# A GLU and linear-attention kernel on one core: the opening in a written order, with products of four blocks first

## The chip, the cores and the metric

One core of a Trainium2 chip runs the whole program. The metric is the device time of one execution in microseconds; lower is better. The core has five instruction streams: TensorE (PE, with its weight loads as PEld), VectorE (DVE), ScalarE (ACT), GpSimd (POOL) and SyncE (SP), which here only issues DMAs. Each stream runs its instructions strictly in order and waits on semaphores of the others.

## The reference, cut to what matters

```python
S, D, H, F = 2048, 1024, 32, 3584                  # float32 throughout
xn = layernorm(x)                                  # mean and variance over D, no weights
# branch A: linear attention with a learned feature map (per head, 32 wide)
q, k, v = split(xn @ wqkv)
phi_q = concat(softmax(q @ w_phi), softmax(-(q @ w_phi)));  phi_k = the same of k
o = (phi_q @ (phi_k.T @ v)) / (phi_q @ sum(phi_k) + 1e-6)
s = o @ wo
# branch B: gated linear unit
h = silu(xn @ w1) * (xn @ w3)
g = silu(h @ w2)
out = x + s * g
```

## The kernel before

The program begins with branch B's first product, xn against w1 and w3. It has two token halves of 1024 tokens; w1 and w3 are cut into 28 blocks of 128 columns (`NF`). One token half against one column block is a **block** k (0 to 55; 0 to 27 are the first half). Each block is a 2 by 2 matrix product (two groups of 512 tokens by two halves of the 1024 features, against w1 and w3), done in Winograd's form with seven products instead of eight. The A operands are A11, A12 (the features of the first 512 tokens), A22, and the sums S1 to S4 of the four quarters; the B operands are B11, B21, B22 and the sums T1 to T4 (`ORDER`).

Every operand is held as two fp32r parts, the rounded value (high, a cast on ACT) and the rest (low, a subtraction on DVE): `split`, L93 and L94 in the trace. A product is 12 matmuls of 128x512 (`PASSES`: high by high, high by low, low by high, for four slices of the features). So nothing can be multiplied before ACT has made its high parts and DVE its low parts.

PSUM has three kinds of banks for the products: b (A11, S2, S3, A22 of a block), a (A11's partner A12) and c (S1, S4); `evict` takes them out on ACT and DVE. A fourth kind, tag `tr`, serves the turns and folds.

**The opening** must make all seven A operands of the first half out of eight x tiles: load (`load_x`, L189), statistics (`stats`, L195 and L196, then `rstd`: a square root on ACT and five small DVE steps), normalization in place (`norm`, L214), **turns** (`turn`: four transposes on PE into PSUM, L219, copied out by ACT, L224), sums (`a_sums`, L231 to L237 on DVE), splits. Tiles 0 to 3 give A11 and A12, tiles 4 to 7 the other quarters.

**Folds** (`fold`, L248) multiply the transposed wk and wq with the block-diagonal w_phi (`bd`), so that later the features come out of one product. There are 32; each is a load (`load_w`, L241), four narrow matmuls on PE, an ACT copy and a store to DRAM (L312, L313). They need neither x nor DVE. 22 of them stand in the opening (`first_folds`), ten are side work.

A scheduler orders the opening; from step 4 of the product list `seq` the program's own order holds (`in_order`). Steps are products. `stage` sets at which step a block's B quarters are loaded and summed on POOL (`b_sums`, L129 and L130, then two more subtractions), `LEAD` splits an operand four steps ahead of its product, and `at`, `side_x`, `side_fold`, `side_kv` and `side_store` hang side work on steps: the second half's x, the remaining folds, the weights of branch A. The pool `q` of 11 rooms of 512 KB passes from x tiles to B operands.

The first products before are

```python
seq[:10] = [(0, "A11"), (0, "A12"), (1, "A11"), (1, "A12"), (0, "S2"), (0, "S1"), (0, "S3"), (0, "S4"), (1, "S2"), (0, "A22")]
```

Of the kernel before, what the change touches and what calls it, by code (L numbers as in the profile page):

```python
# [8 lines left out]
F = mybir.dt.float32  # L9
# [19 lines left out]
def tile_kernel(ctx: ExitStack, tc: tile.TileContext, x, wkT, wqT, wv, wphi, wo, w1, w3, w2, out):  # L29
# [116 lines left out]
    BANKS = {"a": 1, "b": 3, "c": 1}  # L146
# [51 lines left out]
    def rstd(mv):  # L198

        sd = small.tile([P, 4, 2], F, name="sd")  # L200
        var = mv[:, :, 1]
        nc.scalar.activation(sd[:, 0], var, AF.Sqrt, bias=eps_t)
        nc.vector.reciprocal(sd[:, 1], sd[:, 0])
# [12 lines left out]
    def turn(half):  # L216
        pt = ps.tile([P, 4, P], F, name="pt", tag="tr", bufs=3)
        for k in range(4):
            nc.tensor.transpose(pt[:, k, :], half[:, k * P:(k + 1) * P], ident)  # L219
        return pt  # L220
# [23 lines left out]
    def fold(wr, c):  # L244

        pw = ps.tile([P, 4, P], F, name="pw", tag="tr", bufs=3)
        for g in range(4):
            nc.tensor.matmul(pw[:, g, :], wr[:, g], bd[:, 4 * c + g, :], start=True, stop=True)  # L248
        return pw
# [9 lines left out]
    def b_operands(rw, bo):  # L259
        b11, b21, b12, b22 = (rw[:, a, h] for a in range(2) for h in range(2))  # L260
        t2 = work.tile([P, 512], F, name="t2", tag="w")
        b_sums(b11, b12, b22, t2)
        yield
        for _, _, n in ORDER:
            src = {"B11": b11, "B21": b21, "T2": t2, "T1": b11, "T3": b12, "B22": b22, "T4": b21}[n]
            bo[n] = quad("bo")
            split(bo[n][:, 0], bo[n][:, 1], src.rearrange("p (k n) -> p k n", n=P))
            if n == "B11":
                nc.gpsimd.tensor_sub(b11, b22, t2)
            elif n == "B21":  # L270
                nc.gpsimd.tensor_sub(b21, b21, t2)
            yield


    phi_raw = flat(blk("phi")[:, :2]).rearrange("p (g f) -> p g f", f=DH)
    nc.sync.dma_start(phi_raw, wphi.rearrange("(g p) f -> p g f", p=P))
# [12 lines left out]
    for n in ("B11", "B21", "B22", "B12"):
        b_load(1, rws[1], n)  # L290
# [3 lines left out]
    for j in range(4):  # L294
        sl = slice(32 * j, 32 * j + 32)
        nc.gpsimd.tensor_copy(bd[sl, :, sl], phi_raw[sl, :, :])
    b_gen = b_operands(rws[0], bo)
    next(b_gen)

    def first_split(n, q, src):  # L300
        sl = slice(q * P, (q + 1) * P)
        split(ao[n][:, 0, :, sl], ao[n][:, 1, :, sl], src)

    at_fold = 0

    def first_folds(n):
        nonlocal at_fold
        for _ in range(n):
            wT, k, c, d = folds[at_fold]
            wr = early_w.pop(0) if early_w else load_w(wT, k, c, work.tile([P, 4, P], F, name="wr", tag="w"))  # L310
            pw = fold(wr, c)
            nc.scalar.copy(wr, pw)  # L312
            nc.sync.dma_start(d, flat(wr))  # L313
            at_fold += 1
# [3 lines left out]
    for t in range(4):  # L318
        stats(mvs[t // 2], t % 2, xs[t])
    for p in range(2):  # L320
        sd = rstd(mvs[p])
        for j in range(2):
            norm(mvs[p], sd, j, xs[2 * p + j])
    for q in range(4):
        raw[q]["A11"] = raw_x(turn(xs[q][0]))
        first_split("A11", q, raw[q]["A11"])
        if q == 1:
            next(b_gen)
# [12 lines left out]
    next(b_gen)
    for q in range(4):
        if q % 2 == 0:
            sd = rstd(mvs[2 + q // 2])
            for j in range(2):
                norm(mvs[2 + q // 2], sd, j, xs[4 + q + j])
        raw[q]["A21"] = raw_x(turn(xs[4 + q][0]))
        raw[q]["A22"] = raw_x(turn(xs[4 + q][1]))
        a_sums(raw[q], nc.vector)
        first_split("S2", q, raw[q]["S2"])  # L350
        first_split("S1", q, raw[q]["S1"])
        if q == 2:
# [149 lines left out]
    FIRST_STEP, HALF = 7, 7 * NF  # L502
    for i in range(4, 8):
        side_x(i, FIRST_STEP + 16 * (i - 4))
    for m in range(at_fold, len(folds)):
        side_fold(m, FIRST_STEP + 6 * (m - at_fold))
    for m in range(9):
        side_kv(m // 4, m % 4, FIRST_STEP + 62 + 11 * m)
# [37 lines left out]
    def stage(k):

        c, r = 7 * k - 4, raw_of(k)
        if k > 1:
            for n, ahead in (("B11", 10), ("B12", 8), ("B22", 6), ("B21", 4)):  # L550
                at(c - ahead, lambda n=n: b_load(k % NF, rws[k % 2], n), sums)
        at(c - 3, lambda: b_sums(r["B11"], r["B12"], r["B22"], wk[4]), sums)
        at(c - 2, lambda: nc.gpsimd.tensor_sub(r["B11"], r["B22"], wk[4]), sums)
        at(c, lambda: nc.gpsimd.tensor_sub(r["B21"], r["B21"], wk[4]), sums)

    def operand(k, n):

        r = raw_of(k)
        src = {"B11": r["B11"], "B21": r["B21"], "T2": wk[4], "T1": r["B11"], "T3": r["B12"], "B22": r["B22"], "T4": r["B21"]}[n]
        bos[k, n] = quad("bo")  # L560
        split(bos[k, n][:, 0], bos[k, n][:, 1], src.rearrange("p (k n) -> p k n", n=P))

    def evict(step, k, an, pb):
# [3 lines left out]
        h0, u0, u1, h1, even = h0s[k % 2], wk[2], wk[3], wk[f % 2], wk[0]  # L567
        if an == "A11":
            nc.scalar.copy(h0, pb)  # L569
# [24 lines left out]
    for k in range(1, 2 * NF):  # L594
        stage(k)

# [17 lines left out]
    for step, (k, an) in enumerate(seq):  # L614
        if step == 4:
            in_order(ENG.PE, ENG.Activation, ENG.DVE, ENG.Pool, ENG.SP)
        tb, f = divmod(k, NF)
        for do in before.pop(step, ()):
            do()
# [5 lines left out]
        for kk in range(4):  # L625
            for u, w in PASSES:
                nc.tensor.matmul(bank, bt[:, w, kk], aos[tb][an][:, u, kk], start=an in ("A11", "A12", "S1") and n == 0,  # L627
                                 stop=LAST[b] == an and n == 11, skip_group_check=True)
                n += 1
        for do in sums.pop(step, ()):  # L630
            do()
        if step + LEAD < len(seq):
            k2, an2 = seq[step + LEAD]
            if k2 and (k2, OPERAND[an2]) not in bos:
                operand(k2, OPERAND[an2])
        for do in after.pop(step, ()):
            do()
        with tc.high_priority() if step < 4 else nullcontext():
            evict(step, k, an, bank)
# [709 lines left out]
```

## Time and profile before

| | us |
|---|---|
| median of 3 runs (lowest, highest) | 2362.84 (2361.11, 2365.02) |
| profiled execution, its time | 2365.4 |
| profiled execution, its span from first to last instruction | 2363.2 |
| PE busy / DVE / ACT / POOL in the span | 2331.2 / 1746.7 / 859.4 / 761.5 |
| first PE instruction | 12.52 |
| PE runs without a gap from about | 72 |

The granted TensorE clock is 1.000 over the span. In the rows of a timeline stand start, duration, engine, line, operation, tile written from tile read, shape, count, and in brackets how long the engine was idle before and what ended that. Rows merged with xN show the time from the first one's start to the last one's end. PE's records overlap by their pipeline, so the distance between starts, not the duration of one, is its pace.

### The profile page before, as it was taken

How to read it: one execution, taken by the hardware profiler on the slowest of the kernel's cores; microseconds unless marked ns; L12 is line 12 of the kernel's file. 1: busy time of each engine (PE TensorE's matmuls, PEld its weight loads, DVE VectorE, ACT ScalarE, POOL GpSimd, SP SyncE). 2: the span in 40 equal slices, each digit the busy share in tenths (PEclk: the TensorE clock that was granted, in tenths of full speed). 3: DMA queues.
4: the chain of work that ended last, by engine and by line, in shares of the span. 5: the costliest groups of instructions: out<-in, count | busy, mean ns of one | idle time of the engine just before them, and what ended most of it. 6: DMA issues, size and time to landing. Idle time of an engine off the chain costs nothing.

```text
span 2363.2 us, 35867 instructions
## 1 busy us (share of the span) xinstructions
PE 2331.2 (99%) x13298; PEld 1923.2 (81%) x13298; DVE 1746.7 (74%) x2539; ACT 859.4 (36%) x1534; POOL 761.5 (32%) x569
## 2 busy tenths in 40 slices
PE   6999999999999999999999999999999999999999
PEld 5788888888788888888888888888888888888877
DVE  8567788775688888885476555798688777888883
ACT  6445555443344444543222111234422222243100
POOL 1233555552355555552000000231011111115872
PEclk9999999999999999999999999999999999999999
DMA  7667789877877778776999877999445443377753
GB/s 264 201 213 239 229 294 308 288 249 223 261 274 264 260 255 282 258 272 216 386 327 334 321 251 261 349 349 330 154 139 180 178 178 110 125 256 289 250 184 134
DMA packets 319406, 586.83 MB, mean 248 GB/s; under 512 B 25600, under 2 KB 158208, under 8 KB 316544
## 3 DMA queue, kind: packets, MB, share of 16 engines
q1 hardware_dynamic: 304448, 569.87, 69.8%
q10 hardware_dynamic: 14784, 14.68, 1.8%
q8 instruction: 105, 1.72, 0.3%
q14 instruction: 69, 0.57, 0.1%
HBM read 379.19 MB, written 205.79 MB: 248 GB/s over the span
## 4 chain that ended last, share of the span: by engine, by line
PE 93%; DMA 3%; DVE 2%; issue 1%; ACT 1%; SPq 0%; POOL 0%; POOLq 0%; ACTq 0%; DVEq 0%
PE bankb L627 25%; PE bankb L1087 13%; PE bankc L627 13%; PE bankb L681 9%; PE pm L1214 7%; PE bankc L1087 6%; PE banka L627 6%; PE bankc L681 5%; PE banka L1087 3%; PE banka L681 2%; DMA e_d<-eq 1%; PE po L1058 1%; PE pkv L666 1%; PE pw L248 1%; DMA xoA<-xo_d0A 0%
## 5 line engine op out<-in xcount | busy, mean ns | idle before, releaser
L94 DVE TENSOR_TENSOR bo<-rw,bo 128x512 fp32r<-128x512 f32 x336 | 310.1, 923 | 154.0 <-ACT bo L93 152.4
L1097 POOL TENSOR_TENSOR acc<-acc,u 128x512 f32<-128x512 f32 x48 | 64.5, 1343 | 448.8 <-ACT u L1096 427.8
L93 ACT CAST bo<-rw 128x512 fp32r<-128x512 f32 x336 | 201.2, 617 | 4.1 <-POOL room L129 2.0
L1087 PE MATMUL bankb<-bo,as 128*128 128x512 f32 x816 | 200.9, 389 | 0.0
L1087 PEld LDWEIGHTS bankb<-bo,as 128*128 128x128 f32 x816 | 153.1, 188 | 32.0 <-DVE acc L1099 0.2
L1214 PE MATMUL pm<-wos,oT 128*128 128x512 f32 x720 | 166.9, 390 | 0.0
L627 PE MATMUL bankb<-op0A,bo 128*128 128x512 f32 x672 | 164.1, 391 | 0.7 <-DVE op0A L94 0.7
L627 PE MATMUL bankb<-op0S,bo 128*128 128x512 f32 x672 | 163.0, 391 | 0.0
L627 PE MATMUL bankc<-op0S,bo 128*128 128x512 f32 x672 | 163.0, 391 | 0.0
L627 PE MATMUL bankb<-op1S,bo 128*128 128x512 f32 x672 | 161.5, 389 | 1.1 <-ACT h L569 1.1
L627 PE MATMUL bankc<-op1S,bo 128*128 128x512 f32 x672 | 161.5, 389 | 1.0 <-ACT bo L93 1.0
L627 PE MATMUL bankb<-op1A,bo 128*128 128x512 f32 x672 | 161.4, 389 | 0.0
L1214 PEld LDWEIGHTS pm<-wos,oT 128*128 128x128 f32 x720 | 134.6, 188 | 30.5 <-issue 2.9
L627 PEld LDWEIGHTS bankb<-op1S,bo 128*128 128x128 f32 x672 | 126.0, 188 | 27.7 <-ACT h L569 1.6
L627 PEld LDWEIGHTS bankc<-op1S,bo 128*128 128x128 f32 x672 | 126.0, 188 | 27.5 <-ACT bo L93 1.4
L627 PEld LDWEIGHTS bankb<-op1A,bo 128*128 128x128 f32 x672 | 126.1, 188 | 26.2
L627 PEld LDWEIGHTS bankb<-op0A,bo 128*128 128x128 f32 x672 | 125.4, 188 | 26.4 <-DVE op0A L94 0.9
L627 PEld LDWEIGHTS bankc<-op0S,bo 128*128 128x128 f32 x672 | 125.5, 188 | 25.7
L627 PEld LDWEIGHTS bankb<-op0S,bo 128*128 128x128 f32 x672 | 125.3, 188 | 25.6
L1087 PE MATMUL bankc<-bo,as 128*128 128x512 f32 x576 | 146.2, 389 | 0.0
L129 POOL TENSOR_TENSOR rw<-rw 128x512 f32<-128x512 f32 x56 | 83.1, 1484 | 136.1 <-DMA rw<-in_w 110.5
L1087 PEld LDWEIGHTS bankc<-bo,as 128*128 128x128 f32 x576 | 108.1, 188 | 22.5
(246 smaller groups left out, 4694.7 us busy)
## 6 DMA issues: line engine op xcount, KB each, us to landing
rw<-in_w SPq DMA_DIRECT2D x224, 256.0 KB, 3.5
hr<-h_d SPq DMA_DIRECT2D x56, 512.0 KB, 4.0
xoS<-xo_d0S SPq DMA_DIRECT2D x48, 512.0 KB, 8.7
xoS<-xo_d1S SPq DMA_DIRECT2D x48, 512.0 KB, 6.7
xoA<-xo_d0A SPq DMA_DIRECT2D x36, 512.0 KB, 6.5
xoA<-xo_d1A SPq DMA_DIRECT2D x36, 512.0 KB, 6.4
e<-e_d SPq DMA_DIRECT2D x32, 512.0 KB, 5.9
h_d<-h SPq DMA_DIRECT2D x56, 256.0 KB, 4.0
```

Source lines behind the costliest of these rows:

```text
L93: nc.scalar.copy(hi, src)
L94: (by or nc.vector).tensor_sub(lo, src, hi.bitcast(F))
L129: nc.gpsimd.tensor_sub(b12, b22, b12)
L248: nc.tensor.matmul(pw[:, g, :], wr[:, g], bd[:, 4 * c + g, :], start=True, stop=True)
L627: nc.tensor.matmul(bank, bt[:, w, kk], aos[tb][an][:, u, kk], start=an in ("A11", "A12", "S1") and n == 0, stop=LAST[b] == an and n == 11, ...
L666: nc.tensor.matmul(pkv[sl, m], e[:, m // 4, (m % 4) * P + 32 * h:(m % 4) * P + 32 * h + 32], v[:, 4 * (m % 4) + h], start=first and m == 0 ...
L681: nc.tensor.matmul(bank[b], xo[an][:, u, k], wb[bn][:, w, k], start=an in ("A11", "A12", "S1") and n == 0, stop=LAST[b] == an and n == 11, ...
L1058: nc.tensor.matmul(po[a][32 * j:32 * j + 32, 256 * c:256 * c + 256], kvt[sl, c, j, s], ets[c, j // 2][sl, 2 * (j % 2) + s].rearrange("p t ...
L1087: nc.tensor.matmul(bank[b], t[:, u, pos + k], bos[kb, bn, k][:, w], start=first and n == 0, stop=LAST[b] == an and n == 5, skip_group_chec ...
L1097: nc.gpsimd.tensor_add(c, c, u)
L1214: nc.tensor.matmul(p, oT[a][k // 4][:, u, k % 4], wos[c, 4 * (k % 2) + k // 2][:, w], start=n == 0, stop=n == 23)
```

## The change

Everything from the first statistics to step 13 is now written out by hand in one order for all five engines.

- `OPENING` puts eight products with A11 and A12 of blocks 0 to 3 first, then six of blocks 0 and 1. Bank b gets four buffers instead of three, `tr` two instead of three. The other products keep their order.
- B11 and B21 of blocks 0 to 3 are loaded early, in between the x tiles; w_phi is loaded behind x. Tiles 4 to 7 and S1, S3 use rooms of operands that are made later.
- `hi` and `lo` are the two halves of a split, apart; `bhi` and `blo` the same for a B operand; `st`, `root`, `rstd` and `nm` the statistics, the square root, the small steps and the norm; `products(step)` the 12 matmuls of a step, `out_of(step)` its eviction.
- `raw_x` of A21 is gone: `first_sums` reads that turn straight from PSUM.
- Silu of the four early gate sums is put off (`finish_h0`); those of blocks 2 and 3 are spilled to DRAM and fetched at steps 18 and 20.
- 6 folds are left in the opening; 26 are side work from step 14, one in six steps. Side work starts at step 14 instead of 7.

```diff
-    BANKS = {"a": 1, "b": 3, "c": 1}
+    BANKS = {"a": 1, "b": 4, "c": 1}
...
-        pt = ps.tile([P, 4, P], F, name="pt", tag="tr", bufs=3)
+        pt = ps.tile([P, 4, P], F, name="pt", tag="tr", bufs=2)
...
+    in_order(ENG.PE, ENG.Activation, ENG.DVE, ENG.Pool, ENG.SP)
+    for t in range(4):
+        xs.append(load_x(t, whole()))
+    raw23 = [quad("wx", F).rearrange("p u k t -> p u (k t)") for _ in range(2)]
+    for n in ("B11", "B21"):
+        for k in range(2):
+            load_early_b(k, n)
...
+    for t in range(4, 8):
+        xs.append(load_x(t, [x_room[:, t - 4, h] for h in range(2)]))
+    for k in (2, 3):
+        for n in ("B11", "B21"):
+            load_early_b(k, n)
+        if k == 2:
+            b_load(0, rws[0], "B22")
+            b_load(0, rws[0], "B12")
     nc.sync.dma_start(phi_raw, wphi.rearrange("(g p) f -> p g f", p=P))
+    b_load(1, rws[1], "B22")
+    b_load(1, rws[1], "B12")
...
+    def hi(n, *qs):
+        for q in qs:
+            nc.scalar.copy(place(n, q, 0), raw_at(n, q))
+    def lo(n, *qs):
+        for q in qs:
+            nc.vector.tensor_sub(place(n, q, 1), raw_at(n, q), place(n, q, 0).bitcast(F))
...
+    def first_half(n, *qs):
+        for q in qs:
+            raw[q][n] = raw_x(turn(xs[q][n == "A12"]))
+            hi(n, q)
+    def other_turns(q):
+        raw[q]["A22"] = raw_x(turn(xs[4 + q][1]))
+        return turn(xs[4 + q][0])
+    def first_sums(q, pt):
...
+        nc.vector.tensor_add(raw[q]["S1"], pt, raw[q]["A22"])
+        nc.vector.tensor_sub(raw[q]["S3"], raw[q]["A11"], pt)
...
-    FIRST_STEP, HALF = 7, 7 * NF
+    FIRST_STEP, HALF = 14, 7 * NF
...
-        side_kv(m // 4, m % 4, FIRST_STEP + 62 + 11 * m)
+        side_kv(m // 4, m % 4, FIRST_STEP + 62 + 10 * m)
...
+    OPENING = [(0, "A11"), (1, "A11"), (0, "A12"), (2, "A11"), (1, "A12"), (3, "A11"), (2, "A12"), (3, "A12"),
+               (0, "S1"), (0, "S2"), (0, "S3"), (1, "S2"), (0, "A22"), (0, "S4")]
+    seq = OPENING + [m for m in seq if m not in OPENING]
...
+    st(0)
+    st(1)
+    sds[0] = root(mvs[0])
...
+    first_half("A11", 0)
+    first_half("A12", 0)
+    st(3)
+    sds[1] = root(mvs[1])
...
+    first_half("A11", 2, 3)
+    lo("A11", 0, 1, 2, 3)
+    products(0)
+    bhi(1, "B11")
+    first_half("A12", 2, 3)
...
+    products(7)
+    pt3 = other_turns(3)
+    first_sums(3, pt3)
+    hi("S1", 0, 1, 2, 3)
...
```

Three places show how the instructions stand. The names in them: `pt` is a turn's PSUM tile, `pw` a fold's, `xf` a turned quarter in SBUF, `op0A` and `op0S` are A operands, `bo` a B operand, `h` a block's gate, `rw` and `wx` raw B quarters, `x_room` the tiles 4 to 7, `s_room` the raw sums S1 and S3.

PE before, from its first instruction on: folds and turns lie between single products' matmuls.

```order
L219 MATMUL pt<-ident,xt 128x128 x16
L248 MATMUL pw<-bd,wr 128x128 x8
L219 MATMUL pt<-ident,xt 128x128 x8
L627 MATMUL bankb<-op0A_298,bo 128x512 x2
L219 MATMUL pt<-ident,xt 128x128 x4
L627 MATMUL bankb<-op0A_298,bo 128x512
L219 MATMUL pt<-ident,xt 128x128 x4
L248 MATMUL pw<-bd,wr 128x128 x4
L627 MATMUL bankb<-op0A_298,bo 128x512 x5
```

PE now, from its first instruction to the first folds: whole products and turns alternate.

```order
L223 MATMUL pt<-ident,xt 128x128 x24
L682 MATMUL bankb<-op0A_296,bo 128x512 x12
L223 MATMUL pt<-ident,xt 128x128 x8
L682 MATMUL bankb<-op0A_296,bo 128x512 x12
L682 MATMUL banka<-op0A_297,bo 128x512 x12
L682 MATMUL bankb<-op0A_296,bo 128x512 x12
L223 MATMUL pt<-ident,x_room 128x128 x8
L682 MATMUL banka<-op0A_297,bo 128x512 x12
L682 MATMUL bankb<-op0A_296,bo 128x512 x12
L223 MATMUL pt<-ident,x_room 128x128 x8
L682 MATMUL banka<-op0A_297,bo 128x512 x12
L223 MATMUL pt<-ident,x_room 128x128 x8
```

The eight turns of x_room's first tile moved behind four products, the folds behind eight.

DVE before, at the normalization of tiles 4 to 7 (`xt` there):

```order
L571 TENSOR_TENSOR h_854<-banka,h_854 128x512
L214 TENSOR_SCALAR xt<-xt,mv,sd 128x512 x6
L231 TENSOR_TENSOR s_571<-xf 128x512
L214 TENSOR_SCALAR xt<-xt,mv,sd 128x512
L233 TENSOR_TENSOR xf<-xf 128x512
```

DVE now, from the first statistics of tile 4 to the norms of tiles 4 and 5:

```order
L195 BN_STATS st<-x_room 128x6 x2
L196 BN_AGGR mv<-st 128x2
L342 TENSOR_TENSOR bo<-wx,bo 128x512
L195 BN_STATS st<-x_room 128x6 x2
L196 BN_AGGR mv<-st 128x2
L342 TENSOR_TENSOR bo<-wx,bo 128x512
L207 RECIPROCAL sd<-sd 128x2
L209 TENSOR_TENSOR sd<-sd 128x2
L210 SCALAR_TENSOR_TENSOR sd<-mv,sd 128x2
L211 TENSOR_SCALAR sd<-sd 128x2
L212 TENSOR_TENSOR sd<-sd 128x2
L624 TENSOR_TENSOR h_308<-banka,h_308 128x512
```

The norms of tiles 4 and 5 (four L218) follow these; the low parts of block 2's B operands and a gate's add moved ahead of them.

ACT now, around products 9 and 10, where S3's high parts (`op0S_300` from `s_room`) are made:

```order
L405 COPY wr<-pw 128x512
L318 CAST op0S_300<-s_room 128x4x128 x2
L628 COPY wk_305<-bankb 128x512
L318 CAST op0S_300<-s_room 128x4x128 x2
L338 CAST bo<-rw 128x512
```

The copy L628 takes a finished product out of bank b; two of the four casts stand behind it.

More of the change, by code (lines that the diff above doesn't have):

```diff
@@ L293, in tile_kernel, with place @@
     nc.gpsimd.memset(bd, 0.0)
[L294 to L314, printed above, removed]
+    def place(n, q, u):
+        return ao[n][:, u, :, q * P:(q + 1) * P]
@@ L316, in tile_kernel, with b_third, st @@
+    def b_third(k):
+        r = raw_of(k)
+        nc.gpsimd.tensor_sub(r["B21"], r["B21"], raw_b(k, "T2"))
     mvs = [small.tile([P, 2, 2], F, name="mv", bufs=4) for _ in range(4)]
     raw = [{} for _ in range(4)]
-    for t in range(4):
+    sds = {}
+    def st(t):
         stats(mvs[t // 2], t % 2, xs[t])
[L320 to L328, printed above, removed]
@@ L593, in tile_kernel @@
     sums, evens = {}, [None]
-    for k in range(1, 2 * NF):
+    for k in range(2, 2 * NF):
         stage(k)
+    for j, step in enumerate((18, 20)):
+        at(step, lambda j=j: nc.sync.dma_start(h0s[j], hs_d[j]), sums)
+    at(14, lambda: operand(2, "T2"), sums)
     def fetches(tb, steps):
@@ L612, in tile_kernel, with products @@
         at(END_AT + (-6, -4, -2, 0, 1, 2, 3)[j], lambda n=n: xo.update(reload(0, [n])), sums)
[L614 to L619, printed above, removed]
+    def products(step):
+        k, an = seq[step]
+        tb = k // NF
         b = BANK[an]
@@ new lines, in tile_kernel @@
+    st(3)
+    sds[1] = root(mvs[1])
+    rstd(mvs[1], sds[1])
+    nm(2)
+    nm(3)
+    first_half("A11", 1)
+    first_half("A12", 1)
+    blo(0, "B11")
+    first_half("A11", 2, 3)
[3 more added lines that the diff above has]
+    first_half("A12", 2, 3)
+    lo("A12", 0, 1)
+    blo(1, "B11")
+    products(1)
+    bhi(0, "B21")
+    bhi(1, "B21")
+    lo("A12", 2, 3)
+    blo(0, "B21")
+    products(2)
+    blo(1, "B21")
+    b_first(0)
+    b_second(0)
+    b_third(0)
+    for j in range(4):
+        sl = slice(32 * j, 32 * j + 32)
+        nc.gpsimd.tensor_copy(bd[sl, :, sl], phi_raw[sl, :, :])
@@ new lines, in tile_kernel @@
+    out_of(0)
+    st(4)
+    bhi(2, "B11")
+    blo(2, "B11")
+    products(3)
+    out_of(1)
+    st(5)
+    bhi(2, "B21")
+    blo(2, "B21")
+    load_fold()
+    sds[2] = root(mvs[2])
+    rstd(mvs[2], sds[2])
+    out_of(2)
+    nm(4)
+    nm(5)
+    pt0 = other_turns(0)
+    products(4)
+    bhi(3, "B11")
+    st(6)
+    blo(3, "B11")
+    out_of(3)
+    first_sums(0, pt0)
+    products(5)
+    pt1 = other_turns(1)
+    st(7)
+    sds[3] = root(mvs[3])
+    bhi(3, "B21")
+    out_of(4)
+    first_sums(1, pt1)
@@ new lines, in tile_kernel @@
+    bhi(1, "T2")
+    blo(1, "T2")
+    b_second(1)
+    b_third(1)
+    products(11)
+    ao["A22"] = slot(0, 6)
+    hi("A22", 0, 1, 2, 3)
+    bhi(0, "T4")
+    lo("A22", 0, 1)
+    out_of(10)
+    lo("A22", 2, 3)
+    blo(0, "T4")
+    b_load(2, rws[0], "B21")
+    f4 = next_fold()
+    products(12)
+    last_sums()
+    ao["S4"] = slot(0, 5)
+    hi("S4", 0, 1, 2, 3)
+    bhi(0, "B22")
+    copy_fold(f4)
+    lo("S4", 0, 1, 2, 3)
+    blo(0, "B22")
+    b_load(2, rws[0], "B22")
+    bhi(1, "T1")
@@ L630, in tile_kernel @@
+    f5 = next_fold()
+    products(13)
+    blo(1, "T1")
+    out_of(12)
+    b_first(2)
+    bhi(1, "T3")
+    blo(1, "T3")
+    copy_fold(f5)
+    out_of(13)
+    out_of(11)
+    bhi(1, "B22")
+    blo(1, "B22")
+    for step in range(len(OPENING), len(seq)):
+        for do in before.pop(step, ()):
+            do()
+        products(step)
         for do in sums.pop(step, ()):
@@ L637, in tile_kernel @@
             do()
-        with tc.high_priority() if step < 4 else nullcontext():
-            evict(step, k, an, bank)
+        out_of(step)
     for step in sorted(after):
```

235 lines of the change are left out of this document (154 added, 81 removed).

## Prediction

> **What bounds the kernel now.** I read the page's parts 1 and 2 first. TensorE is busy for 99% of the span, and only the first of 40 slices (59 us each) shows a 6 for it:
>
> ```profile
> PE 2331.2 (99%) x13298; PEld 1923.2 (81%) x13298; DVE 1746.7 (74%) x2539; ACT 859.4 (36%) x1534; POOL 761.5 (32%) x569
> ...
> PE   6999999999999999999999999999999999999999
> ```
>
> So the opening is the place where an order can win or lose. There I read stretches, then PE's groups up to 72 us, PE's timeline and the chain:
>
> ```profile
> 0.00:72.00 72.00, 49.75 (x313) 42.07 (x314) 57.83 (x117) 46.24 (x87) 16.07 (x21) 1.00 0.77 261
> 72.00:200.00 128.00, 128.00 (x609) 106.95 (x608) 82.05 (x122) 60.94 (x106) 45.39 (x33) 1.00 0.63 197
> ```
> ```profile
> L248 PE MATMUL pw<-bd,wr 128*128 128x128 f32 x176 | 24.7, 289 | 6.6 <-DMA wr<-in_wkT 4.6 <-DMA wr<-in_wqT 1.9
> L219 PE MATMUL pt<-ident,xt 128*128 128x128 f32 x64 | 10.9, 313 | 15.0 <-DVE xt L214 15.0
> L627 PE MATMUL bankb<-op0A,bo 128*128 128x512 f32 x24 | 7.6, 419 | 0.7 <-DVE op0A L94 0.7
> ...
> L627 PE MATMUL bankb<-op0S,bo 128*128 128x512 f32 x13 | 3.9, 413 | 0.0
> L627 PE MATMUL bankc<-op0S,bo 128*128 128x512 f32 x12 | 3.7, 415 | 0.0
> ```
> ```profile
> 77.56 5.44 PE bankb L627 x24
> ...
> 85.72 0.89 PE pw L248 x8
> ...
> 100.24 0.44 PE pt L219 x4
> ```
> ```profile
> 12.52 1.09 PE L219 MATMUL pt<-ident,xt 128*128 128x128 f32 x4 [12.52 <-DVE xt L214]
> ...
> 17.16 2.09 PE L219 MATMUL pt<-ident,xt 128*128 128x128 f32 x8 [0.79 <-DVE xt L214]
> ...
> 21.88 1.04 PE L219 MATMUL pt<-ident,xt 128*128 128x128 f32 x8
> ...
> 71.94 2.91 PE L627 MATMUL bankb<-op0S,bo 128*128 128x512 f32 x12
> ```
>
> Columns of a stretch: PE, weight load, DVE, ACT, POOL busy (instructions), clock, DMA share, GB/s. The unit I count in is **lost PE time**: the clock on the wall less the PE work done, at PE's own pace. The chain gives the pace: a product of 12 matmuls 2.72, a fold of 8 records 0.89, a turn of one half tile 0.44. At 71.94, from where PE runs without a gap, before has done 16 turns (64 records), 22 folds (176) and 72 wide matmuls, six products (24 each to banks b and a with op0A, 12 each to b and c with op0S, one of the 13 being later): 7.0 + 19.6 + 16.3 = 42.9 us. Lost: 71.9 - 42.9 = **29.0 us**. 12.5 of it is the time to the first normalized tile; the rest is waits and half pace (8 turns took 2.09 at 17.16 and 1.04 at 21.88). All PE work is the same in both kernels, so the new time is the old one plus the difference of lost time.
>
> **What the order costs DVE.** Every A operand costs DVE a low part, every B operand another, x costs stats and norms. Rows for the prices:
>
> ```profile
> 8.42 1.23 DVE L195 BATCH_NORM_STATS2 st<-xt 128x6 f32<-128x512 f32 x2
> ...
> 9.82 0.64 DVE L195 BATCH_NORM_STATS2 st<-xt 128x6 f32<-128x512 f32 x1
> ...
> 11.83 3.83 DVE L214 TENSOR_SCALAR xt<-xt,mv,sd 128x512 f32<-128x512 f32 x4
> ...
> 12.25 1.27 POOL L129 TENSOR_TENSOR rw<-rw 128x512 f32<-128x512 f32 x1 [6.70 <-DMA rw<-in_w]
> ...
> 15.58 0.15 DVE L203 RECIPROCAL sd<-sd 128x2 f32<-128x2 f32 x1
> ...
> 16.56 1.91 DVE L214 TENSOR_SCALAR xt<-xt,mv,sd 128x512 f32<-128x512 f32 x4
> ```
> ```profile
> 59.78 2.49 DVE L94 TENSOR_TENSOR op0S<-xf,op0S 128x512 fp32r<-128x512 f32 x4
> ```
> ```profile
> 32.66 2.18 ACT L93 CAST bo<-rw 128x512 fp32r<-128x512 f32 x4
> ```
> ```profile
> 120.68 1.73 POOL L231 TENSOR_TENSOR s<-xf 128x512 f32<-128x512 f32 x1
> 121.19 1.77 DVE L94 TENSOR_TENSOR bo<-rw,bo 128x512 fp32r<-128x512 f32 x1
> ...
> 129.62 0.69 DVE L94 TENSOR_TENSOR bo<-wk,bo 128x512 fp32r<-128x512 f32 x1
> ```
>
> A tile's stats take 1.4 (8.42 to 9.82), the five small steps of rstd 1.0 (15.58 to 16.56), a norm 0.48, a DVE add or subtraction 0.60 in a row, an ACT copy or cast 0.53. Beside POOL's 128x512 instructions the same subtraction took 1.77 instead of 0.69, and four norms 3.83 instead of 1.91.
>
> **The change, step by step.** I lay the written order out with these prices; "lost" is the running sum.
>
> (a) *w_phi goes behind x.* This frees SP and the DMA engines ahead of x:
>
> ```profile
> 0.74 0.45 SPq L276 DMA_DIRECT2D phi<-in_wphi  x1
> 1.25 3.88 SPq L189 DMA_DIRECT2D xt<-in_x  x8
> ```
> ```profile
> 0.00:8.00 8.00, 0.00 (x0) 0.00 (x0) 2.67 (x6) 1.28 (x1) 3.16 (x11) 1.00 0.74 226
> 8.00:19.00 11.00, 4.04 (x16) 3.02 (x17) 10.65 (x28) 3.49 (x8) 2.59 (x2) 1.00 1.05 402
> ```
>
> The issue slot alone is 0.5; the bytes and small packets are bounded by about 1.5 together; I take 1.0. The third tile is then through its stats at 8.8 instead of 9.82, rstd ends at 9.8, and the first turn runs at 10.4 instead of 12.52. phi itself is wanted by the first fold, now near 58 us, long after.
>
> (b) *Up to the first product.* DVE: norms to 11.7, stats of tile 3 to 13.1. The square root for tiles 2 and 3 now stands on ACT behind two copies and two casts of the first turns (11.5 to 13.9), so DVE idles 1.1; rstd ends at 15.2, four norms at 17.1, B's low part at 17.7, three low parts of A11 at 19.5. About 19 us the 24th transfer of 256 KB lands (6.3 MB; the two stretches above moved 1.8 + 4.4 MB by 19.0), and POOL starts the sums of block 0. The fourth low part waits beside them: 1.8, to 21.4. Product (0,A11) can go on only then; 6 turns and two matmuls are done by then, 3.1 us. Lost 18.4. Its clock is taken as half for the first 2 us, which puts its end near 24.2: lost 18.9.
>
> (c) *Next three products* wait 0.7 in all (A12's last turns come behind the first product on PE). Lost 19.6, end 34.0.
>
> (d) *Turns of x4* come before product 4, and on DVE stand behind 2 low parts, stats of two tiles, 2 more low parts, rstd, the add of (0,A12): 29.2 + 1.4 + 0.6 + 1.4 + 1.3 + 1.0 + 0.6, then two norms of 1.6 to 1.7 beside POOL's sums of block 1: 39.0. PE idles 5.0 (without POOL 2.5). Lost 24.6.
>
> (e) Products 4 to 6 run through to 48.9; the turns of x6 wait for its norm, 10.9 of DVE's time after 39.0 (four norms 1.9, stats of two tiles 2.8, a low part 0.6, an add 0.6, four sums 2.4, rstd 1.0, and 1.5 of waiting for the copy of a turn that comes behind product 5): 1.0. Then (3,A12) wants the only bank a; the add that frees it stands on DVE behind two norms, a low part and two sums (with it 3.4, to 53.3), and PE has two turns meanwhile: 2.5. Lost 28.1.
>
> (f) The last tile's turns come behind that product on PE (56.1), and DVE idles 4.2 for them and the copy, to 57.4. Then two sums, four low parts of S1 and T1's make 4.2: (0,S1) runs at 61.7 while PE had turns and two folds: 2.8. Lost 30.9.
>
> (g) S2: an add, four sums, five low parts, 6.0 against a product and a fold: 2.4. S3: half of its casts stand on ACT behind the copy of S2's result, DVE idles 2.4 again: 2.2. Lost 35.5.
>
> (h) (1,S2) and A22 are ready in time. For S4's product DVE needs 16 instructions (9.6) and a 0.7 wait from 73.8: 0.8. (1,S1) then wants bank c, released by two DVE instructions: 1.0. **Lost 37.3** near 88 us, with 14 products done where before had six at 71.9; from there LEAD supplies operands four steps ahead.
>
> (i) *16 folds as side work.* 16 x 0.89 = 14.2 us of PE lie no longer beside waits; that is inside the count, since they are undone work at 88 us, as eight more products are done work. Their copies and DMAs lie beside PE:
>
> ```profile
> 140.00:200.00 60.00, 29.59 (x50) 1.00 0.62 196
> ```
>
> (ACT alone, 60 us, half idle.) If this cover failed, each of the 26 later folds could hold PE by one copy, up to 0.6 each, 15 us; nothing in that row suggests it. I take nothing. The spill of h0 of blocks 2 and 3 (two stores, two loads) and the earlier loads of blocks 2 to 4 cost nothing either: each is wanted two steps or more after its issue. SP waits with the first store for that Silu, near 60; behind it stand the loads for folds 4 and 5, wanted near 79. (g)'s T2 of block 2 is the tightest: last B22 load after 84, some 4 us to land, two POOL instructions, two splits, ready near 92; wanted at 96. The fourth bank b could take away the second of these waits (us in total, times, longest):
>
> ```profile
> PE pw L248 <- DMA wr<-in_wkT: 4.6, 4, 1.5
> ...
> PE bankb L627 <- ACT h L569: 1.1, 1, 1.1
> ```
>
> Its ends are 0 and 1.1; I take 0, since it is one wait, and ACT is what it names. The bank is taken from the buffers of turns and folds, three before and two now: that is the last rival.
>
> **Sum.** 37.3 - 29.0 = +8.3. The profiled execution took 2365.4 with a span of 2363.2, and 2362.84 is the median of the runs, which I use: **2371.1 us**.
>
> [...] Full pace came in the row of 21.88 after work without a long gap from 17.16, 4.3 us later. [...]
>
> **Rivals.**
> *The gap in (d) cools the clock.* Half pace for another 4.3 us loses 2.2 of work, and the turns of x5 stand behind product 5, so DVE's list slips too: 2371.1 + 2.2 = 2373.3. For it speaks the half pace at 17.16, against it, that no row shows it: before's longest wait behind the first tiles is the 1.5 above.
>
> *Holds are mild.* If POOL never holds DVE, (b) gives 1.2 and (d) 2.5 back, and a warm clock from the start 1.1: 37.3 - 4.8 = 32.5, +3.6: 2366.4. For it: POOL's records may overlap DVE less than I lay them; against it the 1.77 row.
>
> *Faster: DVE is not what paces the opening.* If after the gap in (d) every operand is ready, and the gap is the 2.5 of no POOL, lost time stays at 22.1: -6.8, 2356.0. For it: up to product 3 the layout loses only 7 us after its first turn, and the DMA waits of folds (6.5 in the groups) are gone. Against it: 57.83 of 72 us of DVE were busy before, and now DVE has eight more B parts by its list's end. It decides where DVE's list up to B22's low part ends 13 us earlier than my 84.2.
>
> *Side folds collide.* Turns and folds share two buffers instead of three; ten holds of 0.6: 2377. Against it, ACT's idle half.
>
> **How the numbers follow.** Forecast 0.45, cooled clock 0.20, mild holds 0.20, faster 0.08, side folds 0.07. A change within 0.2% (4.7 us, about what a measurement here can tell) is the mild case: 0.20. Slower is 0.45 + 0.20 + 0.07 = 0.72, faster 0.08. The range takes mild holds with another 3 us off, 2363, to the colliding folds, 2377; it leaves out the faster case and half of the last.
>
> **What would show it.** Right: first PE row near 10.4; first wide matmul between 19 and 21; a PE gap of 2 to 5 us near 36 released by L218's norm of x_room; a wait on bank a near 51 to 53; waits on low parts of S1, S2, S3 between 58 and 75; PE without a gap only from about 88. Wrong: PE gapless from before 75, or waits on fold loads or pw copies after step 14.

## The result: slower, by twice the forecast

The changed kernel takes 2380.44 us in the median (2378.9 to 2381.18) against 2362.53 for the kernel before: ratio 1.0074, 95% interval 1.0056 to 1.0091, so +17.9 us where +8.3 was forecast and 2377 was the upper end. The direction was right, the size was not, and the first rival's cause (a clock that cools, given 0.20) was at work: the granted clock stood at 0.50 in two places of the opening.

The profiled execution of the changed kernel took 2378.9 us with a span of 2376.8, its fastest run; the one of before (2365.4) was slower than all four runs of its median, so these two spans differ by 13.6 us only. PE's timeline of the changed kernel over the opening (start, duration, engine, line, operation, tiles, count, and in brackets the idle time ahead and what ended it):

```profile
11.09 4.01 PE L223 MATMUL pt<-ident,xt 128*128 128x128 f32 x16 [11.09 <-DVE xt L218]
...
20.05 4.89 PE L682 MATMUL bankb<-op0A,bo 128*128 128x512 f32 x12 [1.55 <-ACT op0A L318]
...
31.83 2.88 PE L682 MATMUL bankb<-op0A,bo 128*128 128x512 f32 x12
39.65 1.94 PE L223 MATMUL pt<-ident,x_room 128*128 128x128 f32 x8 [4.94 <-DVE x_room L218]
41.24 4.54 PE L682 MATMUL banka<-op0A,bo 128*128 128x512 f32 x12
45.62 2.89 PE L682 MATMUL bankb<-op0A,bo 128*128 128x512 f32 x12
...
52.95 1.06 PE L223 MATMUL pt<-ident,x_room 128*128 128x128 f32 x8 [0.79 <-DVE x_room L218]
56.26 3.00 PE L682 MATMUL banka<-op0A,bo 128*128 128x512 f32 x12 [2.25 <-DVE wk L624]
...
63.49 0.50 PE L682 MATMUL bankc<-op0S,bo 128*128 128x512 f32 x1 [0.61 <-ACT bo L338]
64.71 4.37 PE L682 MATMUL bankc<-op0S,bo 128*128 128x512 f32 x11 [0.72 <-DVE bo L342]
68.92 1.05 PE L252 MATMUL pw<-bd,wr 128*128 128x128 f32 x8
69.72 0.48 PE L682 MATMUL bankb<-op0S,bo 128*128 128x512 f32 x1
70.73 2.80 PE L682 MATMUL bankb<-op0S,bo 128*128 128x512 f32 x11 [0.52 <-DVE bo L342]
...
75.76 0.50 PE L682 MATMUL bankb<-op0S,bo 128*128 128x512 f32 x1 [1.34 <-ACT bo L338]
...
91.14 1.16 PE L682 MATMUL bankc<-op0S,bo 128*128 128x512 f32 x4 [0.88 <-DVE wk L634]
```

Nearly every wait of the layout is there, in its place: the first turn at 11.1 (10.4 forecast), the gap of 4.94 ahead of x4's turns (5.0), 0.79 at x6 (1.0), 2.25 for bank a (2.5), 1.34 at S3. What the layout did not have stands in the durations: the product at 41.24 took 4.54 and the eleven matmuls at 64.71 took 4.37, where the other products behind the first one take 2.8 to 3.0. The stretches say why (PE, weight load, DVE, ACT, POOL busy, then the granted clock, DMA share, GB/s):

```profile
0.00:36.00 36.00, 20.37 (x80) 15.43 (x80) 28.25 (x54) 15.38 (x28) 12.21 (x17) 1.00 0.66 237
36.00:44.00 8.00, 4.35 (x15) 3.80 (x16) 7.84 (x15) 1.59 (x3) 2.69 (x3) 0.61 0.01 2
44.00:65.00 21.00, 16.15 (x85) 12.84 (x84) 12.87 (x27) 9.46 (x17) 0.00 (x0) 0.99 0.06 18
65.00:69.00 4.00, 4.00 (x12) 3.10 (x12) 4.00 (x8) 2.95 (x5) 0.00 (x0) 0.57 0.88 300
69.00:91.00 22.00, 18.48 (x93) 14.64 (x91) 17.17 (x28) 13.77 (x26) 0.55 (x1) 1.00 0.30 103
```

Twice the granted clock fell in mid-opening: it stands at 0.50 from 38 to 44 us and from 66 to 68, and the two stretches above that hold the falls have a mean of 0.61 and 0.57.

Lost PE time at 91.14, with 14 products, 16 turns and 6 folds done (38.1 + 7.0 + 5.3 = 50.5 us): **40.6** instead of the forecast 37.3, and 29.0 before.

### The profile page after: what moved, and what is told of

Read it like the earlier page. It is cut to its first block, busy times and chain, and to the rows that moved or that the text cites. A ratio compares the mean times of both kernels' runs of the same rounds, so it can differ in the third digit from the quotient of the medians.

```text
span 2376.8 us, 35860 instructions
## 1 busy us (share of the span) xinstructions
PE 2338.6 (98%) x13298; PEld 1927.6 (81%) x13298; DVE 1756.6 (74%) x2539; ACT 857.3 (36%) x1530; POOL 762.7 (32%) x569
## 4 chain that ended last, share of the span: by engine, by line
PE 90%; DVE 3%; DMA 3%; issue 1%; ACT 1%; SPq 1%; POOL 0%; DVEq 0%; ACTq 0%; POOLq 0%
PE bankb L682 23%; PE bankb L1309 13%; PE bankc L682 12%; PE bankb L903 9%; PE pm L1436 7%; PE bankc L1309 6%; PE banka L682 6%; PE bankc L903 5%; PE banka L1309 3%; PE banka L903 2%; DMA e_d<-eq 1%; PE po L1280 1%; PE pw L252 1%; DVE bo L342 1%; PE pkv L888 1%
## 5 line engine op out<-in xcount | busy, mean ns | idle before, releaser
L682 PEld LDWEIGHTS bankc<-op1S,bo 128*128 128x128 f32 x672 | 126.1, 188 | 27.5 <-ACT bo L338 1.3
L682 PEld LDWEIGHTS bankb<-op1S,bo 128*128 128x128 f32 x672 | 126.1, 188 | 26.6 <-ACT h L622 0.4
L1309 PEld LDWEIGHTS bankc<-bo,as 128*128 128x128 f32 x576 | 108.2, 188 | 22.4
```

The lines of the kernel that those rows point to most:

```text
L1309: nc.tensor.matmul(bank[b], t[:, u, pos + k], bos[kb, bn, k][:, w], start=first and n == 0, stop=LAST[b] == an and n == 5, skip_group_chec ...
```

## The experiments

### The clock and the gap: two runs with work put into PE's gaps

e1_busy_gap puts 36 small transposes, which nobody reads, into the first gap. e7_busy_two puts 12 more into the second.

```diff
+    def keep_busy(n):
+        pt = ps.tile([P, 4, P], F, name="pt", tag="tr", bufs=2)
+        for k in range(n):
+            nc.tensor.transpose(pt[:, k % 4, :], ident, ident)
...
+    keep_busy(36)
     pt0 = other_turns(0)
...
+    keep_busy(12)            # e7_busy_two only
     products(7)
```

> The changed kernel with 36 transposes of the identity into a turn's PSUM tile, read by nobody, in PE's gap of 4.9 us before the turns of x4. Theory (the gap cools the clock, and the half pace of 39.6 to 44.3 us delays DVE's list, which waits for the turns behind product 5): the granted clock stays 1.00 through 50 us, products 4 and 5 take 2.72 each, and the time falls by 2 to 3 us, to about 2377.5. Rival (DVE paces the opening, PE's slack hides the half pace): clock 1.00 but the time within 1 us of 2380.4. Rival (the clock falls for another cause): clock still 0.5 near 40.

Measured: 2374.61, ratio to before 1.0055 [1.0041, 1.0068], 5.8 us below the changed kernel, more than the 2 to 3 us of the theory. The clock stayed at 1.00 through 50 us and the product behind x4's turns took 3.0 instead of 4.54. But one fall came later, in the timeline of this kernel:

```profile
49.75 1.06 PE L223 MATMUL pt<-ident,x_room 128*128 128x128 f32 x8 [0.83 <-DVE x_room L218]
53.07 4.58 PE L682 MATMUL banka<-op0A,bo 128*128 128x512 f32 x12 [2.25 <-DVE wk L624]
```
```profile
50.00:53.50 3.50, 1.25 (x10) 1.00 0.00 0
```
```profile
53.00:54.00 1.00, 0.93 (x4) 0.89 0.00 0
54.00:55.00 1.00, 1.00 (x4) 0.50 0.00 0
...
56.00:57.00 1.00, 1.00 (x4) 0.50 0.00 0
57.00:58.00 1.00, 1.00 (x8) 0.90 0.00 0
```

PE was never idle for longer than 2.25 us there; it was busy for 1.25 of the 3.5 us up to 53.5, and the clock fell within half a microsecond behind that, to 0.50. S1 now ran at full pace (11 matmuls in 2.83), and S2 waited 1.8 us for its operands where it had waited 0.52:

```profile
67.27 0.50 PE L682 MATMUL bankb<-op0S,bo 128*128 128x512 f32 x1 [0.46 <-ACT bo L338]
69.11 2.77 PE L682 MATMUL bankb<-op0S,bo 128*128 128x512 f32 x11 [1.34 <-DVE bo L342]
```

So the clock is not the whole of the 5.8 us. In the two profiles the product at 91.14 runs at 89.45 here, 1.7 us earlier, and half of that is an earlier first turn (10.24 for 11.09). The spans differ by 5.9; the other 4.2 lie behind the opening, where the two kernels run the same instructions.

> The changed kernel with 36 small PE transposes in the gap ahead of the turns of the first later x tile (as in e1_busy_gap), and 12 more in the 2.3 us that the eighth product waits for bank a. In e1_busy_gap the clock fell once, in that second gap, and the eighth product took 4.6 us in place of 2.9. Theory 'clock': the granted clock is 1.00 from 20 to 100 us, the eighth product takes 2.9 to 3.0 us, and the time is 1 to 2.5 us below that of e1_busy_gap: 2372 to 2373.6. Rival 'DVE paces': the slow product was cover for DVE's work behind it, the wait moves to the next operand, and the time stays at 2374 to 2375; or the clock falls at another place, the same time.

Measured: 2375.77 [1.0042, 1.0067]: no gain over e1_busy_gap shows, as the rival had it, though the two intervals leave room for the 1 to 2.5 us of the theory. The eighth product ran at full pace (3.04), and the fall moved on to S1 (a mean clock of 0.83 from 60 to 70 us):

```profile
54.59 3.04 PE L682 MATMUL banka<-op0A,bo 128*128 128x512 f32 x12 [0.39 <-DVE wk L624]
...
61.86 0.49 PE L682 MATMUL bankc<-op0S,bo 128*128 128x512 f32 x1 [0.62 <-ACT bo L338]
63.08 4.38 PE L682 MATMUL bankc<-op0S,bo 128*128 128x512 f32 x11 [0.72 <-DVE bo L342]
```

From x4's turns to the product that closes the opening (89.47) this profile took 49.1 us, e1_busy_gap's 50.7, since S2 waited only 0.51 behind the slow S1; a start that was 1.6 us later at x4's turns took that back. So the clock of this half-busy opening fell in one place or another (a mean of 0.83 from 50 to 60 us in e1_busy_gap, from 60 to 70 here), and filling a gap was no cure while others stayed.

### DVE's order: one run with two pieces moved

e8_reorder is e1_busy_gap, its 36 idle transposes included, with two pieces moved.

```diff
-    products(7)
     pt3 = other_turns(3)
     first_sums(3, pt3)
+    products(7)
...
     hi("S3", 0, 1)
+    hi("S3", 2, 3)
     out_of(9)
     f3 = next_fold()
-    hi("S3", 2, 3)
```

> e1_busy_gap with two pieces of the written order changed: the turns and sums of the last x tile ahead of the eighth product, and the last two S3 casts on ACT ahead of the copy of S2's result. By the trace of the changed kernel DVE stands still 4.2 us behind the first and 2.2 us behind the second. Theory 'steps (f) and (g)' of the prediction: both idle times go, S1 is ready some 4 us earlier, PE's work becomes gapless 3 to 6 us earlier than in e1_busy_gap (89.5 us), and the time is 2368.5 to 2372. Rival 'another operand is late next' (the early operands of B on DVE and ACT): less than 1.5 us comes back, 2373 to 2375.

Measured: 2369.58 [1.0018, 1.0042], 5.0 us below e1_busy_gap; the theory holds. S1 ran at 58.13 instead of e1_busy_gap's 61.87, without a wait, and the product that runs at 91.14 in the changed kernel and at 89.45 in e1_busy_gap ran at 84.80. Behind 30 us one fall was left, at S2 (`64.08`, 11 matmuls in 4.37; a mean clock of 0.83 from 60 to 70 us, 1.00 in the other stretches).

### POOL's sums, and 32 bytes

e2_pool_later lets POOL wait, by a copy of 16 bytes, until tile 7's statistics, so that the sums of block 1 no longer lie beside DVE's work ahead of x4.

```diff
     st(7)
+    hold = small.tile([P, 2, 2], F, name="hold", bufs=1)
+    nc.gpsimd.tensor_copy(hold, mvs[3])
```

> The changed kernel with one small POOL copy of tile 7's statistics ahead of the sums of block 1, so that these start near 45 us and not at 33. Theory (POOL holds DVE's T of block 2, two of rstd's small steps and a norm for 1.0 each and so makes 3 to 4 us of the 4.9 us gap, which then cools the clock): the gap before the turns of x4 falls to 1 to 2 us, the clock stays at 1.00 there, and the time falls by 4 to 6 us, to about 2375. Rival (the gap is DVE's own list): gap still over 4 us, time within 1 us of 2380.4.

Measured: 2397.95 [1.0139, 1.0167], 17.5 us *more* than the changed kernel; no theory had that. Its opening was as expected: the gap ahead of x4 fell from 4.94 to 1.63, and PE was gapless some 2 us earlier. The loss lay far behind it, in matmuls that each took longer (busy, mean ns). Changed kernel, then this one:

```profile
L1309 PE MATMUL bankb<-bo,as 128*128 128x512 f32 x816 | 201.0, 389 | 0.0
L1309 PE MATMUL bankc<-bo,as 128*128 128x512 f32 x576 | 146.2, 389 | 0.0
```
```profile
L1311 PE MATMUL bankb<-bo,as 128*128 128x512 f32 x816 | 204.1, 393 | 0.0
L1311 PE MATMUL bankc<-bo,as 128*128 128x512 f32 x576 | 148.7, 393 | 0.0
```

By my count the new tile of 16 bytes takes 32 of each partition among the small tiles and moves every tile of the pools behind them by 32 bytes (no trace shows an address). Two runs test that: e5_pool_pad has the same copy and takes the 32 bytes from a pad; e6_before_32B is the kernel before with 32 bytes more of pad and nothing else.

```diff
-PAD = 32
+PAD = 24                     # e5_pool_pad, with the copy of e2_pool_later
...
+PAD = 40                     # e6_before_32B, in the kernel before
```

> The run with POOL held back until st(7) (e2_pool_later) opened about 2 us better than the changed kernel and still took 17.5 us more; its 128x512 products run slower everywhere behind 700 us (a product with the third operand 389 ns in the changed kernel, 393 to 396 there). Theory 'place': the added 16-byte tile, which takes 32 bytes, moved every tile that lies behind the small ones by 32 bytes, and the matmuls read their operands slower there. Here the same copy stands, and the pad of the small tiles is 32 bytes smaller, so that all the others lie where they lay in the changed kernel: 2376 to 2380, the matmuls at 389 ns again. Theory 'POOL': the later POOL work itself costs the 17 us by a wait that the trace does not name: 2395 to 2400 again.

> The kernel before, and nothing but 32 bytes more of pad, which move the same tiles by 32 bytes. Theory 'place': 13 to 21 us slower than before, 2375 to 2384, with matmuls of 393 to 396 ns where before has 389. Theory 'POOL', or a fault of the one kernel: no difference, 2361 to 2364.

Measured: 2378.1 [1.0051, 1.0076] for the first, 2.3 us below the changed kernel and back near its level, with the first group above at 389 ns again, and 2384.39 [1.0078, 1.0106] for the second, 22.4 us above before (a little more than forecast). The place alone costs 0.9%. In the same stretch, 1600 to 2200 us, the same number of matmuls of branch B's second product (h against w2) kept PE busy for 533.7 us before and 544.7 with the 32 bytes; of before and of e6_before_32B:

```profile
1600.00:2200.00 600.00, 533.73 (x2352) 1.00 0.56 195
```
```profile
1600.00:2200.00 600.00, 544.70 (x2352) 1.00 0.54 190
```

The granted clock is 1.00 in both, so it is not the cause. Why the matmuls take longer was not isolated. The changed kernel has the same pad as before, and the same matmuls take 389 ns in both, so none of its 17.9 us comes from this. And POOL's holds turn out to be worth little by themselves: of the 3.3 us that e5_pool_pad takes off the gap at x4, a new wait of 2.38 at x6 (DVE waits for a copy, then two small steps of the next `rstd` beside POOL's sums take 0.68 and 1.20 for 0.16) and a fall of the clock at the product of 51.37 (5.46 us; a mean of 0.66 from 50 to 60) take most back.

### One part alone, on the kernel before

e3_phi_only: only w_phi's load is put behind x tiles 0 to 3.

> The kernel before with w_phi's load moved behind x tiles 0 to 3, nothing else. Theory (the move brings the first statistics, and all that follows them, forward by 0.5 to 1.5 us): first turn near 11.5 instead of 12.52, time 2361 to 2362. Rival (the later fold loads and folds set the end of the opening): first turn earlier, but the time within 0.5 us of 2362.5, since the waits for fold loads grow by what the start gains.

Measured: 2360.57, ratio 0.9997 [0.9988, 1.0006]: no difference that shows; (a)'s 1.0 us is within what the interval allows. But its first turn ran at 12.86, not near 11.5 (12.52 and 12.81 in before's two profiles). The first statistics began at 3.34 in place of 4.68, but by the first norm that lead was gone (12.04 for 11.83). So (a)'s gain is not shown, nor its 1.5 for bytes and small packets, and the changed kernel's earlier first turn (11.09) can't be put down to w_phi's move alone.

e4_folds_side and e10_before_six: before's order with 6 and with 16 opening folds; the others are side work.

```diff
-        first_folds(2)
+        first_folds(1 if q == 0 else 0)      # e4_folds_side
...
             first_split(n, q, raw[q][n])
-        first_folds(3)                       # none left in e4_folds_side
+        first_folds(1)                       # e10_before_six, and only this
```

> The kernel before with 6 folds in the opening and 26 as side work from step 7, nothing else. Theory (folds filled PE time that DVE leaves open, so taking 16 x 0.89 = 14.2 us of them out shortens the opening by less than that): the opening's lost time rises from 29.0 to 35 to 41 and the time by 6 to 12 us, to 2369 to 2375. Rival (the opening before is held by the loads and copies of its folds, 6.5 us of waits for loads in PE's groups): the opening ends earlier by the 14.2 and those waits, and the time is unchanged or falls, 2356 to 2363.

Measured: 2373.09 [1.0036, 1.0061], 11.3 us more. PE has nothing else to do in these holes: it waits 21.0 us for normalized tiles instead of 15.0, and the clock is down, at 0.50 from 50 to 60 us and a mean of 0.82 from 60 to 70.

```profile
PE pt L219 <- DVE xt L214: 21.0, 5, 12.6
PE bankb L626 <- ACT op0S L93: 7.8, 1, 7.8
```

> The kernel before with 16 opening folds for 22: each of the last three stages folds one in place of three, and six more are side work. The trace of before shows seven waits of PE on fold loads there, 6.4 us together. Theory 'folds fill PE time that DVE leaves open' (e4_folds_side: 16 moved, 11.3 us more, 0.7 each): 3 to 5.3 us slower, 2365 to 2367.5. Rival 'those folds wait for their loads and hold the products behind them': 0 to 4 us faster, 2358 to 2362.

Measured: 2363.37, ratio 1.0007 [0.9998, 1.0016]. Six folds cost about 1 us in the median, 0.2 each, not 0.7: between the two theories, and the interval includes no difference at all. These six stand where PE waited for loads in before; they are among the 16 of e4_folds_side, whose other ten by the difference of the medians cost 10 us, more than the 0.89 each of their own work.

### Everything mended, and both kernels once more

e9_all takes the changed kernel and e8_reorder's two pieces, without any idle transposes, and moves what its rows name: x6's norms ahead of x5's sums, POOL held until these norms (with the pad made smaller), S3's operand of B ahead of a copy on ACT, a fold into S2's wait, a fold into bank c's.

```diff
+    st(7)
+    sds[3] = root(mvs[3])
     products(5)
     pt1 = other_turns(1)
-    st(7)
-    sds[3] = root(mvs[3])
     bhi(3, "B21")
     out_of(4)
-    first_sums(1, pt1)
     rstd(mvs[3], sds[3])
     nm(6)
     nm(7)
+    hold = small.tile([P, 4], F, name="hold", bufs=1)
+    nc.gpsimd.tensor_copy(hold, xs[7][1][:, :4])
+    first_sums(1, pt1)
...
     out_of(8)
+    f3 = next_fold()
     products(9)
...
+    hi("S3", 2, 3)
+    bhi(0, "T3")
+    copy_fold(f3)
     out_of(9)
...
-    f5 = next_fold()
     products(13)
+    f5 = next_fold()
```

> The changed kernel with the written order mended wherever the runs so far show a PE gap in the opening, and without small transposes for cover: the two pieces of e8_reorder; POOL's sums of block 1 held back until the norms of the last x tile, and these norms ahead of the sums of x5 (the gaps before the turns of x4 and x6); S3's operand of B ahead of the copy of S2's result; one fold moved into the wait for S2's operands, one into the wait for bank c; the 32 bytes of the held tile taken from the pad. From the trace of e8_reorder: 3.8 us at the turns of x4, 0.8 at x6, 1.5 to 1.9 at S2 and 1.6 if the clock stays at full there, 0.9 at bank c, 8 us together. Theory 'the order, not the fold count, costs the time': 2360 to 2364, level with the kernel before. Rival 'what is left is DVE's work in one row': about half comes back, 2364 to 2368. Rival 'the clock falls where another short gap is left': 2366 to 2370.

Measured: 2364.67 [1.0000, 1.0018], 0.7 us above the range of the theory and in the lower part of the first rival's. Against the changed kernel's run beside it (e12_after, 2380.75) 16.1 of 18.5 us came back, with the same first products and the same 6 opening folds. The clock stayed at 1.00 from 30 to 100 us; this run does not part what the waits gave from what the clock gave. The product at 91.14 is the last row here:

```profile
36.00 1.07 PE L223 MATMUL pt<-ident,x_room 128*128 128x128 f32 x8 [1.59 <-DVE x_room L218]
36.82 3.02 PE L682 MATMUL banka<-op0A,bo 128*128 128x512 f32 x12
...
59.77 2.79 PE L682 MATMUL bankb<-op0S,bo 128*128 128x512 f32 x11 [0.98 <-DVE bo L342]
63.24 5.74 PE L682 MATMUL bankb<-op0S,bo 128*128 128x512 f32 x24 [0.68 <-ACT wk L628]
...
77.95 2.97 PE L682 MATMUL bankc<-op0S,bo 128*128 128x512 f32 x12
```

The same 50.5 us of PE work at 77.95: lost 27.5, 13.1 less than 40.6. It does not beat the kernel before, which loses 29.0 and, in a second profile, 26.6.

> The kernel before once more, for a second profile. The first one shows 2365.4 us where the median is 2362.5. Theory 'the first profile is a slow execution': 2361 to 2364 in the median, and a span of 2358 to 2361 whose difference to 2363.2 lies in one place. Rival 'a profile costs that much': a span of 2362 to 2364 again.

> The changed kernel once more, beside the others on one chip: 2378 to 2382, 0.65 to 0.85% above before. If the clock falls at the same two places (ahead of the fifth product, and at S1), its span is 2375 to 2379; if it falls at one place more or less from execution to execution, the span differs by 1.5 to 2.6 us for each.

Measured: 2362.29 and 2380.75 (ratio 1.0074 [1.0061, 1.0087]). Before's second profile has a span of 2357.3, 5.9 below the first, so the first was a slow execution. Of that, 2.5 lie in the opening: the folds' loads came earlier, so PE waits 2.2 us for them in place of 6.5, and it is gapless from 69.45 instead of 71.94. The other 3.4 lie behind it.

```profile
PE pw L248 <- DMA wr<-in_wkT: 2.2, 5, 0.9
```
```profile
69.45 2.89 PE L627 MATMUL bankb<-op0S,bo 128*128 128x512 f32 x12
```

The changed kernel's second span is 2378.7. Its clock fell at three places, at the first product, ahead of the fifth and at the eighth, not at S1, and the products there took 5.83 (4.89 in the first profile), 4.96 (4.54) and 5.46 (3.00):

```profile
19.00:25.00 6.00, 5.86 (x14) 0.50 0.85 294
...
39.00:44.50 5.50, 4.64 (x15) 0.50 0.02 3
...
56.00:62.00 6.00, 5.10 (x12) 0.50 0.00 0
```
```profile
19.14 5.83 PE L682 MATMUL bankb<-op0A,bo 128*128 128x512 f32 x12 [1.55 <-ACT op0A L318]
...
41.45 4.96 PE L682 MATMUL banka<-op0A,bo 128*128 128x512 f32 x12
...
56.90 5.46 PE L682 MATMUL banka<-op0A,bo 128*128 128x512 f32 x12 [2.25 <-DVE wk L624]
...
94.40 2.97 PE L682 MATMUL bankc<-op0S,bo 128*128 128x512 f32 x12 [0.88 <-DVE wk L634]
```

Lost: 26.6 before (69.45 - 42.9) and 43.9 after, +17.3.

## Where the prediction was right and where it failed

**The layout, right.** The changed kernel's waits in the opening are those of (d) to (h). The terms count a wait from where the work before it would have ended at PE's pace; so counted, from start to start, x4's gap is 5.1 us (forecast 5.0), x6's 1.1 (1.0), bank a's 2.4 (2.5), S1's with its folds 2.7 (2.8), S3's 2.3 (2.2), S4's 0.8 (0.8) and bank c's 1.2 (1.0). Only S2's was smaller in the first profile, 0.8 for 2.4. (The brackets alone add to 13.5: a lone matmul's row lasts 0.48 where its pace is 0.23, and a bracket begins only at the row's end.) Part of this is luck. (d) came out by two errors that cancel: without POOL beside it the gap is 1.63 (e5_pool_pad) where the layout has 2.5, and POOL held other instructions than the ones named, little of the norms (2.33 for four, where 1.91 is free), but a low part and two steps of `rstd` on two columns:

```profile
33.12 1.69 DVE L342 TENSOR_TENSOR bo<-wx,bo 128x512 fp32r<-128x512 f32 x1
...
35.11 1.11 DVE L210 SCALAR_TENSOR_TENSOR sd<-mv,sd 128x2 f32<-128x2 f32 x1
...
36.46 1.10 DVE L212 TENSOR_TENSOR sd<-sd 128x2 f32<-128x2 f32 x1
37.48 0.68 DVE L624 TENSOR_TENSOR h<-banka,h 128x512 f32<-128x512 f32 x1
38.08 2.33 DVE L218 TENSOR_SCALAR x_room<-x_room,mv,sd 128x512 f32<-128x512 f32 x4
```

(b) came out near in the same way. It lets (0,A11) wait 1.8 for its fourth low part and then run at half pace for 2 us; no idle time stands inside the product's row, and its twelve matmuls took 4.7 us for 2.7, so 19.4 us were lost at its end where 18.9 was forecast. The granted clock stands at 1.00 in the profile there, as it does at the half pace of before's row at 17.16, so it is not shown that these two are the clock. The 2 us at half clock that (b) takes are an assumption that no run shows: in the second profile the clock is 0.50 from 19 to 25 us, over the product's whole 5.83.

Steps (f) and (g), DVE's idle times of 4.2 and 2.2, were shown by e8_reorder: moving the two pieces gave 5.0 us back.

**The clock, the step that failed.** I gave a cooled clock 0.20 and left it out of the sum; as a rival it was one fall behind (d), priced at 2.2. It fell twice in one profile and three times in the other, to 0.50 each time. From start to start at PE's pace, the lost time divides so (us):

| | forecast | first profile | second profile |
|---|---|---|---|
| up to the fourth product's end | 19.6 | 20.1 | 20.4 |
| waits (d) to (h) | 17.7 | 16.4 | 17.9 |
| slow pace behind the fourth product | 0 | 4.1 | 5.6 |
| lost by the changed kernel | 37.3 | 40.6 | 43.9 |
| lost by the kernel before | 29.0 | 29.0 | 26.6 |

The 4.1 are 0.7 at x4's turns (1.59 to the next start, 0.88 at full pace), 1.7 at the fifth product (4.38 for 2.72) and 1.7 at S1 (4.21 to the next start for 2.5). The 5.6 are 0.7 and 2.1 at the same first two, 2.5 at the eighth product and 0.3 at the turns behind it. A fall and a wait can cover each other: in the first profile DVE and ACT made S2's operands while S1 ran slowly, so the clock's net price there is some 2.5; where S1 ran at full pace, in the second profile and in e1_busy_gap, S2 waited its 2.4 (1.8 in the brackets). The argument against that rival, that no row of before shows it, was weak: in before folds stand in the holes, and without 16 of them, in e4_folds_side, the clock stood at 0.50 from 50 to 60 us.

In the prediction's own numbers, the row of 21.88 comes 4.7 us behind 17.16, not 4.3, 32.5 - 29.0 is +3.5 and 22.1 - 29.0 is -6.9; the forecast does not hang on these.

**The base of the subtraction.** 29.0 was read in an execution 2.6 us above before's median; the second profile gives 26.6. The two pairs of profiles give +11.6 and +17.3 for the opening, 14.5 in the mean, against +8.3.

**Step (i), not contradicted.** The side folds were priced at no wait. Outside the opening the spans differ by another 2.0 and 4.1. Part of it is a side fold that waits for its load, which the prediction had named a sign of being wrong:

```profile
PE pw L252 <- DMA wr<-in_wqT: 1.6, 1, 1.6
```

It was 1.1 in the second profile. The rest is not clear of chance. From the product at 91.14 to the last instruction the changed kernel's two profiles take 2285.7 and 2284.3 us; e1_busy_gap, e7_busy_two, e8_reorder and e9_all, which run the same instructions there, take 2281.5, 2282.2, 2283.5 and 2284.9. In the mean of the two pairs 14.5 + 3.0 = 17.5 stands beside the 17.9 and 18.5 between the medians. That the buffers of turns and folds collide (the last rival) is not seen: no row of PE waits for a copy of `pw`.

**The faster rival** did not come. e9_all, with the same eight products first and DVE's list put right, loses 27.5 us in the opening, between the 29.0 and the 26.6 of before, and stays 2.4 us above before in the median. Whether a better order still would pass it is not shown.

## What to carry to other kernels

When PE waits in many short places, count the clock with the waits. Here 22 folds that need no operand from DVE looked like dead weight, and the granted clock of before is 1.00 all through its opening; with 6 of them left, e4_folds_side showed 0.50 from 50 to 60 us, longer waits, and 11.3 us more. With the same 6 and an order that closes the waits, e9_all kept 1.00 from 30 to 100 us and stayed 2.4 us above before. A layout can have every wait right and still miss: the slow pace between the waits cost 4.1 and 5.6 us in the two profiles. Read a baseline from more than one profile before subtracting from it, since an opening that waits on DMAs moved by 2.4 us between two executions here. When an experiment adds a tile, keep every other tile where it was, or the place is what you measure: 32 bytes cost 22.4 us here.

## What the hardware showed that I had not expected

- 32 bytes more of pad among the small tiles, and nothing else: the first group of branch B's second product took 393 ns a matmul in the mean instead of 389, and the kernel before went from 2362.0 to 2384.4 us, 22.4 more.
- The clock fell without a long gap: in e1_busy_gap, to 0.50, just behind 3.5 us in which PE was busy for 1.25, with no idle stretch above 2.25 us. In the changed kernel's first profile 2.48 us busy of the 4 up to 65.0 were followed by a fall to 0.50, 1.75 of the 4 up to 57.0 were not. What sets off a fall these runs do not show.
- Beside POOL's 128x512 sums DVE instructions of 128x2 took about as long as one of 128x512: two took 1.11 and 1.10 us instead of the 0.16 of e5_pool_pad, where POOL stood still, and a low part 1.69 instead of 0.69. An add that reads PSUM beside them took its usual 0.68.
